# Maxima and minima taken off in PSUM by TensorE in the first K phase, with an order planned from separate pitches and latencies

## The chip, the cores and the metric

The kernel runs on one core of a Trainium2 chip. The metric is the device time of one execution in microseconds. Engines are named as the profile names them: PE (TensorE), DVE (VectorE), ACT (ScalarE), POOL (GpSimd). "The kernel before" has a median of 1112.03 us (3 runs, 1111.32 to 1113.44).

## The reference

Two layers of linear attention with a learned feature map, each followed by a gated MLP. Sequence 2048, width D = 576, 32 heads of 18 columns, MLP width 4608, bf16.

```python
def A(x, wqkv, w_phi, wo):                 # x is LayerNormed
    q, k, v = ...                          # x @ wqkv, 32 heads of 18
    pq = einsum("bhsd,hdf->bhsf", q, w_phi); pk = ...   # the same for k
    phi_q = concat([softmax(pq), softmax(-pq)])         # over the 18 columns
    phi_k = concat([softmax(pk), softmax(-pk)])
    kv = einsum("bhsf,bhsd->bhfd", phi_k, v); z = phi_k summed over s
    o  = (phi_q @ kv) / (phi_q @ z + 1e-6)
    return o @ wo
def B(x, w_gate, w_up, w_down):
    return ((x @ w_gate) * (x @ w_up)) @ w_down
x = x + A(ln(x)); x = x + B(ln(x)); x = x + A(ln(x)); x = x + B(ln(x))
```

softmax(-pk) needs the minimum where softmax(pk) needs the maximum. So each tile of 128 rows needs, for each of 32 heads, a maximum, a minimum, two exponentials, two sums, and two products with the reciprocals.

## The kernel before

The kernel folds w_phi into the K and Q weights. It then works on tiles of 128 rows: LayerNorm, transpose, projections of K, V and Q, softmax of K, and products with V that add up in three PSUM banks. After the last K tile, DVE copies that sum through a mask into SBUF (the "masked copy" of the K/V state), and only then can Q tiles be finished. The MLP of layer 1 starts when the first two Q tiles (Q0 and Q1) have gone through the whole attention. Q projections of later tiles can be done early, as filler in idle PE time, or later inside the MLP.

The softmax front of one tile:

```python
def softmax_front(self, st_, pz, Wm, km, crit, ...):
    ...                                       # two PSUM banks, projection on PE
    for h in range(2):                        # ACT copies the tile to SBUF
        ... e.copy(psb[:, pz, 288*h:288*h+288], s.ps[:, bank, 0:288])
    ops = [Op(665, ... tensor_reduce(mxmn[:, pz, 0, :], p3, AX.X, ALU.max))]   # DVE, from SBUF
    for h in range(2):
        ops.append(Op(370, ... tensor_reduce(mxmn[...], pv, AX.X, ALU.min)))   # DVE, from PSUM
    yield ("ops", "dve", ops)
    yield ("alt", [(eng, [Op(dur, ... tensor_tensor(d1, p3, mxb, ALU.subtract))])
                   for eng, dur in (("pool", 1150), ("dve", 675))[:1 + (crit > 1)]])
    ...                                       # two subtractions of the minimum: DVE, from PSUM
    yield from s.softmax_tail(sm, crit, pz)   # 2 exps (ACT), sum (DVE), reciprocal, 2 products:
                                              # the same ("pool", 1150), ("dve", 675) alternatives
```

The order of instructions on each engine is not written down: a list scheduler inside the kernel's Python makes it. Each `Op` carries a price in ns; the scheduler books it on its engine when its inputs are ready by the plan. An engine then runs its instructions in that order, whatever the real durations are. An "alt" may go to the engine where the plan has it done earlier; `crit > 1` (K tiles 14 and 15) adds DVE as an alternative for products that are GpSimd's otherwise.

```python
SEM_LAT = 64.0          # one wait between any two engines
...
    f = self.fin.get(d, 0.0) + (PE_SELF if eng == "pe" and d[0] == "pe" else SEM_LAT)
...
    fin = t + o.dur     # the price, as given in the Op
```

## Time and profile before

I cut the execution into four stretches, by PE's timeline: up to the first gate/up matmul of MLP 1, MLP 1 up to the first Wq matmuls after its last down matmul, the layer boundary up to the first gate/up matmul of MLP 2, and the rest.

| stretch, kernel before | from | to | length, us |
|---|---|---|---|
| first stretch (K phase and first Q tiles) | 0 | 116.65 | 116.65 |
| MLP 1 | 116.65 | 617.40 | 500.75 |
| layer boundary | 617.40 | 650.64 | 33.24 |
| MLP 2 and end | 650.64 | 1109.5 | 458.9 |

PE is full in the MLP stretches. Work taken out of them shortens the time directly.

### The profile page before, as it was taken

The page shows a single profiled execution, that of the slowest core. Times are in us where ns is not written, and L with a number is a line of the kernel's source. Part 1 is how long each engine was busy: PE and PEld are TensorE (multiplying, and loading weights), DVE is VectorE, ACT ScalarE, POOL GpSimd, SP SyncE. Part 2 cuts the span into 40 slices and gives each one's busy share as a digit, 9 for nine tenths or more (in the row PEclk, how much of TensorE's full clock was granted, in tenths as well). Part 3 has the DMA queues.
Part 4 walks back from the last instruction along what each step waited for, and adds up shares of the span by engine and source line. Part 5 has one row for each costly group of instructions (what it writes and reads, how often), then busy time and mean ns, then how long its engine had stood idle before and what let it go on. Part 6 is the DMA issues. An engine that isn't in the chain of part 4 may idle for free.

```text
span 1109.5 us, 33782 instructions
## 1 busy us (share of the span) xinstructions
PE 1072.4 (97%) x15342; PEld 832.2 (75%) x15342; DVE 586.1 (53%) x1192; ACT 373.7 (34%) x855; POOL 311.4 (28%) x330
## 2 busy tenths in 40 slices
PE   6787999999999999999999899999999999999998
PEld 4565886868687786869687678696969696969685
DVE  8998744646375564636453675444435353524231
ACT  6776631414133242404232463131313130402120
POOL 4885512414152432413220252211212130300000
PEclk9999999999999999999999999999999999999999
DMA  7595227273552616371523313727172726262504
GB/s 169 121 279 194 38 44 195 48 205 47 149 100 78 162 29 194 48 204 27 159 69 96 98 24 47 215 36 216 36 215 35 205 47 188 63 182 48 180 26 140
DMA packets 185002, 129.07 MB, mean 116 GB/s; under 512 B 103322, under 2 KB 183706, under 8 KB 183706
## 3 DMA queue, kind: packets, MB, share of 16 engines
q1 hardware_dynamic: 184858, 126.91, 44.6%
q8 instruction: 120, 1.97, 0.7%
q14 instruction: 24, 0.20, 0.1%
HBM read 100.75 MB, written 2.36 MB: 93 GB/s over the span
## 4 chain that ended last, share of the span: by engine, by line
PE 87%; DVE 4%; DMA 1%; ACT 1%; POOL 1%; issue 0%
PE ps L1428 50%; PE ps L1501 22%; PE ps L1002 7%; PE ps L1503 3%; PE ps L990 2%; PE ps L1289 2%; PE ps L1170 1%; DVE ss L1117 1%; POOL dd L1128 1%; DVE x_sb L1364 1%; DMA oT<-dd 1%; DMA wdr<-in_B_w_down_dram 0%; DMA wdx<-in_B_w_down_dram 0%; DVE mxmn L1035 0%; DVE dd L1049 0%
## 5 line engine op out<-in xcount | busy, mean ns | idle before, releaser
L1428 PE MATMUL ps<-xT,Wu 64*128 64x256 bf16 x4608 | 581.8, 269 | 0.0
L1428 PE MATMUL ps<-xT,Wg 64*128 64x256 bf16 x4608 | 579.2, 269 | 0.8 <-ACT xT L972 0.8
L1428 PEld LDWEIGHTS ps<-xT,Wu 64*128 64x128 bf16 x4608 | 431.5, 94 | 22.0 <-DVE hT L1476 0.3
L1428 PEld LDWEIGHTS ps<-xT,Wg 64*128 64x128 bf16 x4608 | 427.4, 94 | 27.4 <-issue 3.3
L1474 ACT CAST hT<-ps 128x512 bf16<-128x512 f32 x288 | 168.4, 585 | 568.5 <-PE ps L1428 541.7
L1476 DVE TENSOR_TENSOR hT<-ps,hT 128x512 bf16<-128x512 f32 x288 | 198.3, 690 | 240.7 <-ACT hT L1474 238.9
L1501 PE MATMUL ps<-wdr,hT 128*128 128x512 bf16 x960 | 245.2, 380 | 1.0 <-DMA wdr<-in_B_w_down_dram 1.0
L1503 PE MATMUL ps<-wdr,hT 128*128 128x64 bf16 x960 | 185.0, 193 | 0.0
L1428 PE MATMUL ps<-xT,Wr 64*128 64x256 bf16 x1152 | 184.9, 269 | 0.0
L1501 PEld LDWEIGHTS ps<-wdr,hT 128*128 128x128 bf16 x960 | 93.9, 98 | 111.1 <-DMA wdr<-in_B_w_down_dram 1.8
L1128 POOL TENSOR_TENSOR dd<-dd,ss 128x576 bf16<-128x576 bf16 x119 | 137.1, 1174 | 123.0 <-ACT ss L1124 119.0
L1099 POOL TENSOR_TENSOR dd<-xT,mxq 128x576 bf16<-128x576 bf16 x56 | 63.5, 1163 | 329.4 <-DVE mxq L1095 329.4
L1544 DVE TENSOR_TENSOR x_sb<-ps,x_sb 128x64 bf16<-128x64 f32 x32 | 7.0, 220 | 228.6 <-PE ps L1503 228.6
L962 POOL TENSOR_SCALAR xln<-x_sb,nmean,rstd 128x576 bf16<-128x576 bf16 x100 | 61.1, 616 | 182.1 <-ACT rstd L951 103.7
L1503 PEld LDWEIGHTS ps<-wdr,hT 128*128 128x128 bf16 x960 | 94.1, 98 | 0.2
L1117 DVE TENSOR_REDUCE ss<-dd 128x64 f32<-128x1152 bf16 x61 | 81.9, 1344 | 15.1 <-ACT dd L1111 15.0
L1428 PEld LDWEIGHTS ps<-xT,Wr 64*128 64x128 bf16 x1152 | 78.1, 94 | 5.2
L1501 PE MATMUL ps<-wdx,hT 128*128 128x512 bf16 x192 | 54.3, 380 | 0.1
L1109 ACT ACTIVATE dd<-dd 128x576 bf16<-128x576 bf16 x61 | 41.7, 684 | 32.8 <-DVE dd L1049 22.7
L1040 POOL TENSOR_TENSOR dd<-psb,mxmn 128x576 bf16<-128x576 bf16 x26 | 30.3, 1166 | 64.8 <-DVE mxmn L1030 64.8
L934 DVE BATCH_NORM_STATS2 st<-x_sb 128x6 f32<-128x288 bf16 x120 | 45.9, 444 | 2.4 <-DMA x_sb<-in_A_x_dram 2.4
L1002 PE MATMUL ps<-Wo,oT 64*128 64x288 bf16 x504 | 44.0, 283 | 1.2 <-DMA oT<-dd 0.4
(123 smaller groups left out, 970.0 us busy)
## 6 DMA issues: line engine op xcount, KB each, us to landing
wdr<-in_B_w_down_dram SPq DMA_DIRECT2D x240, 288.0 KB, 3.7
wdx<-in_B_w_down_dram SPq DMA_DIRECT2D x48, 288.0 KB, 3.7
Wg<-in_B_w_gate_dram SPq DMA_DIRECT2D x4, 1152.0 KB, 17.0
Wu<-in_B_w_up_dram SPq DMA_DIRECT2D x4, 1152.0 KB, 19.5
x_sb<-in_A_x_dram SPq DMA_DIRECT2D x8, 288.0 KB, 3.4
out_dram<-x_sb SPq DMA_DIRECT2D x16, 144.0 KB, 2.7
Wraw<-in_A_wqkv_dram SPq DMA_DIRECT2D x8, 144.0 KB, 2.8
xT<-xln SPq DMA_TRANSPOSE x58, 2.6
```

What stands on the lines that cost most here:

```text
L934: ops.append(Op(d_dve(288), (lambda e, j=j, h=h, src=src: e.bn_stats(st[:, sl[j], 6 * h:6 * h + 6], src)), reads=rd, writes=[("st", sl[j], ...
L962: em = [(lambda e, j=j, a=a, b=b, c=c: e.tensor_scalar(xln[:, sl[j], a:b], x_sb[:, ss[j], c:c + b - a], s.nmean[:, sl[j]:sl[j] + 1], rstd[ ...
L1002: out.append(Op(61, (lambda e, h=h, k=k, st=(i == 0 and k == 0), sp=(i == 1 and k == 3): e.matmul(s.ps[:, banks[h], 0:N], L[r, k, :], Wm[r ...
L1099: yield ("ops", "pool", [Op(1150, (lambda e, d=d, mb=mb: e.tensor_tensor(d, p3, mb, ALU.subtract)), reads=[("xT", st_), ("mq", mq, br)], w ...
L1109: yield ("ops", "act", [Op(590, (lambda e: e.activation(de2, de2, ACTF.Exp, scale=-1.0)), reads=s.ddk(sm, 1), writes=s.ddk(sm, 1))])
L1117: Op(1320, (lambda e: e.tensor_reduce(ss[:, sm, :].rearrange("p (b g) -> p b g", b=2), e4, AX.X, ALU.add)), reads=s.ddk(sm, 0) + s.ddk(sm, ...
L1128: yield ("alt", [(eng, [Op(dur, (lambda e, ev=ev, rb=rb: e.tensor_tensor(ev, ev, rb, ALU.mult)), reads=s.ddk(sm, br) + [("ss", sm)], write ...
L1428: out.append(Op(54.3, (lambda e, bank=bank, cs=cs, lhsT=lhsT, rhs=rhs, st=st, sp=sp: e.matmul(ps[:, bank, cs].rearrange("p (a n) -> p a n" ...
L1474: yield ("ops", "act", [Op(540, (lambda e, gb=gb, p=p: e.copy(hT[:, p, :], ps[:, gb, :])), reads=[("gu", gb)], writes=[("hT", p)] + (s.raw ...
L1476: yield ("ops", "dve", [Op(625, (lambda e, ub=ub, p=p: e.tensor_tensor(hT[:, p, :], ps[:, ub, :], hT[:, p, :], ALU.mult)), reads=[("gu", u ...
L1501: ops = [Op(d_pe(512), (lambda e: e.matmul(s.ps[:, bank, 0:512], lhsT, s.wslot(slot)[:, fi, 0:512], start=(f == 0), stop=(f == NF - 1))), ...
L1503: Op(d_pe(64) + 3, (lambda e: e.matmul(s.ps[:, z, 64 * sl:64 * sl + 64], lhsT, s.wslot(slot)[:, fi, 512:576], start=(f == 0 and (sl == 0 o ...
```

## The change

The intent: DVE is the busiest engine of the first K phase. So for K tiles 0 to 13 the subtraction goes to PE. DVE takes maxima and minima of the K tile straight from PSUM into a 128-column tile `mx`; PE transposes it, ACT or DVE copies it back negated as `mxT`, and PE multiplies it with a constant matrix `E` of zeros and ones and adds that to the K tile in its own PSUM bank: for the first exponential K - max, and, since the second `E` holds the difference of the two patterns, K - min for the second. ACT's exponentials read PSUM. The SBUF copy, the subtractions of DVE and that of GpSimd go. The plan gets separate latencies for each engine, lower prices for ACT, and other knobs.

```diff
-SEM_LAT = 64.0
+LAT = {"pe": 200.0, "act": 145.0, "dve": 120.0, "pool": 90.0, "sp": 64.0}
...
 def d_act(n, psum=False, ptrs=0):
-    return n / 1.2 + (63.0 if psum else 92.0) + 93.0 * ptrs
+    return n / 1.2 + 50.0
...
+        self.pes = (0, 1, 2, 3, 4, 5, 6, 7, 8, 9, 10, 11, 12, 13)
-        self.wage = 0.0
-        self.lnage = 4
-        self.lnlead = 14
+        self.wage = 10
+        self.lnage = -3
+        self.lnlead = 7
-        self.pqp = (5, 5)
-        self.pqg = 12
-        self.NPQ = 2
+        self.pqp = (3, 3)
+        self.pqg = 10
+        self.NPQ = 3
...
+    def pe_front(self, st_, crit):
+        ...                                    # K projection into two PSUM banks
+            yield ("ops", "dve", [Op(370, ... tensor_reduce(s.mx[:, mx, c:c + 16], pv, AX.X, alu)) ...
+        yield ("ops", "pe", [Op(70, ... matmul(tp, s.mx[:, mx, :], s.ident[:], ...))])
+        yield ("alt", [... ("act", ... activation(s.mxT[:, mx, :], tp, ACTF.Copy, scale=-1.0)), ("dve", ...)])
+        for br in range(2):
+            for h in range(2):
+                ... matmul(s.ps[:, bank, 0:288], s.mxT[:, mx, :], s.E[:, br, ...], start=False, ...)
+            for h in range(2):
+                ... activation(s.dd[:, sm, br, ...], s.ps[:, bank, 0:288], ACTF.Exp, scale=1.0 - 2.0 * br)
+        ...                                    # banks released, then the old tail without its exps
```

## The prediction

> **What bounds the kernel now.** I read the page's busy totals first, then a table of busy time in stretches that I cut where the work changes, then the timelines of PE and DVE inside the first stretch. The total:
>
> ```profile
> PE 1072.4 (97%) x15342; PEld 832.2 (75%) x15342; DVE 586.1 (53%) x1192; ACT 373.7 (34%) x855; POOL 311.4 (28%) x330
> ```
>
> TensorE is busy for 97% of the 1109.5 us span, so the change can only win PE's idle time, or PE work. The stretches say where that idle time is. Columns: busy us of PE, PEld, DVE, ACT, POOL with instruction counts, then clock, DMA share and GB/s.
>
> ```profile
> 0.00:116.65 116.65, 89.60 (x760) 64.10 (x762) 101.95 (x221) 82.09 (x219) 75.00 (x84) 0.97 0.65 182
> 116.65:150.00 33.35, 33.19 (x584) 29.47 (x585) 22.96 (x41) 15.47 (x35) 15.46 (x14) 1.00 0.28 47
> 150.00:610.00 460.00, 459.50 (x6896) 354.96 (x6891) 242.27 (x498) 144.50 (x330) 134.12 (x144) 1.00 0.45 110
> 610.00:655.00 45.00, 39.86 (x396) 29.25 (x396) 29.41 (x62) 24.48 (x62) 11.04 (x10) 1.00 0.21 63
> 655.00:1080.00 425.00, 424.50 (x6432) 338.57 (x6430) 183.80 (x364) 104.26 (x206) 75.76 (x80) 1.00 0.45 115
> 1080.00:1109.50 29.50, 25.78 (x288) 15.83 (x284) 5.76 (x10) 2.93 (x5) 0.00 (x0) 0.99 0.43 131
> ```
>
> At 116.65 us the first gate/up matmul of the gated MLP starts (line 1428 in PE's timeline). From there PE is full except for 5.1 us at the layer boundary and 3.7 us at the end. Of 37.1 us of idle PE, 27.0 lie before 116.65. In that first stretch DVE is the busiest, 101.95 of 116.65 us, and between 18.34 us (first maximum of a K tile) and 102.13 us (the masked copy of the K/V state) its timeline has only 5.6 us of gaps. So the first K phase is DVE's. One K tile on DVE:
>
> ```profile
> 45.06 0.74 DVE L1030 TENSOR_REDUCE mxmnx<-psbx 128x32 f32<-128x576 bf16 x1
> 45.72 0.81 DVE L1035 TENSOR_REDUCE mxmnx<-ps 128x16 f32<-128x288 f32 x2
> 46.47 1.35 DVE L1117 TENSOR_REDUCE ss<-dd 128x64 f32<-128x1152 bf16 x1
> 47.74 0.81 DVE L1049 TENSOR_TENSOR dd<-ps,mxmnx 128x288 bf16<-128x288 f32 x2
> 48.47 0.74 DVE L1030 TENSOR_REDUCE mxmnx<-psbx 128x32 f32<-128x576 bf16 x1
> ```
>
> Start to start, not end to start, is what an instruction costs here: 0.66 us for the maximum, 0.73 for two minima, 1.27 for the sum, 0.73 for two subtractions, 3.4 us in all, to which LayerNorm comes. PE's pitches are read in the same way:
>
> ```profile
> 626.98 7.51 PE L990 MATMUL ps<-Wq,xT 128*128 128x288 bf16 x60
> 634.33 0.36 PE L1170 MATMUL ps<-vx,dd 128*128 128x152 bf16 x3
> ...
> 120.59 0.78 PE L1002 MATMUL ps<-Wq,xT 64*128 64x288 bf16 x10
> 121.20 0.27 PE L1428 MATMUL ps<-xT,Wg 64*128 64x256 bf16 x1
> ```
>
> 7.35 us for 60 is 0.1225 us per full-array matmul of 288 columns; 0.61 us for 10 is 0.061 per half-array one.
>
> **What the Trainium skill says.** "VectorE: DVE Perf Modes", the perf-mode tier table, lists tensor_reduce at 1x for every operand kind. The trace agrees: 576 bf16 elements from SBUF at a 0.66 us pitch are 1.15 ns per element, and 288 fp32 from PSUM at 0.365 us are 1.27, so moving the maximum from SBUF to PSUM costs little (0.73 against 0.66). "Perfetto Trace Analysis", identifying the most-contended engine, warns that matmul busy time is no measure of headroom, since matmuls overlap. The trace agrees, ten matmuls of 1.39 us busy start every 1.23 us, so I count PE work in pitches. "TensorE: Matmul & The Clock Gate", what's actually happening, says that PE's clock halves after an idle window of about 3.4 us. The trace agrees: after PE's idle 3.39 us before 32.76 us, ten Wk matmuls took 2.19 us instead of 1.39. Fewer long gaps would therefore also save a little there.
>
> **The change part by part.** It applies to tiles 0 to 13 of layer 1's K; tiles 14 and 15, all Q tiles and layer 2 keep the old front.
>
> DVE loses, per tile, the 0.66 us maximum and two subtractions (0.73), and gets two maxima from PSUM (0.73). Net 0.66 us, times 14: 9.2 us. The 0.73 us of subtraction are not won: they pay for the maxima.
>
> GpSimd loses its subtraction, 1.166 us in the row of line 1040; the built order has 20 of them against 35, so 17.5 us go, and three small set-up operations come, some 3 us while it waits anyway. ACT loses two copies (about 0.29 us pitch) and two 576-wide exponentials (0.58) per tile, and gets four 288-wide exponentials (an estimate from the copies: 0.29 to 0.33) and a 128-wide negation (about 0.2): about even. Neither is the bound at 82 and 75 us.
>
> PE gets, per tile, one 128-wide transpose by matmul (about 0.08 us from the existing transposes, 6 in 0.49) and four 288-wide matmuls: 14 x (0.08 + 4 x 0.1225) = 8.0 us.
>
> The new plan also moves work; this I take from the instruction order of the built kernels. Before the first gate/up matmul the changed kernel has 160 Wq matmuls instead of 110, and three state products of 12 matmuls instead of two. A Q tile costs 10 x 0.1225 = 1.23 us there and 18 x 0.061 = 1.10 us in the MLP, so five tiles and one product (0.62 us) take 6.7 us into the first stretch and 6.1 us out of the saturated one. The whole program has 336 Wq matmuls instead of 392, and a tile moved to the full array saves 8 of them, so seven tiles move: two more in layer 2, 2.2 us out of the saturated MLP, 2.5 us into the boundary or just before it, where 5.1 us of PE are idle; I book a net gain of 1 us.
>
> **The sum for the first stretch.** PE's pitched work from 13.1 us (first V projection) on, before: 454 matmuls of 288 x 0.1225 = 55.6; 16 K/V products x 0.61 = 9.8; state products 1.3; transposes 3.0; folding of Wq 1.6; together 71.3 of 103.55 us, 69%. After: 71.3 + 8.0 + 6.7 = 86.0.
>
> DVE between first K maximum and masked copy, before: 83.8 - 5.6 gaps = 78.2 us. After: minus 9.2, minus one sum of a Q tile that now comes later (1.3), plus one subtraction that the plan gives DVE (1.25), plus a Wq copy and two negations (0.8): 69.8. With the same gaps the masked copy comes 8.4 us earlier, at 93.7. I do not believe in the same gaps. A tile's exponentials now wait for DVE reduce, PE transpose, ACT copy, PE matmul; both PSUM banks are held through all this, and only five banks are free beside the three of the K/V state, so two tiles fill them almost. PE would have to run near 85% in that time. I add 2.5 us: masked copy at about 96.
>
> From there to the MLP, before, it took 14.5 us, with 11.5 us of PE work after the copy. The plan now puts eight Q tiles there instead of four and a third product: 4.9 + 0.6 = 5.5 us more, of which some 1 us falls into gaps of the chain. 96 + 14.5 + 4.5 = 115. So the MLP starts only 1.7 us earlier, but with 6.1 us less to do.
>
> Total: -1.7 - 6.1 - 1 = -8.8 us, from 1112.0 to 1103.
>
> **The rivals.** (a) PE becomes the bound of the first phase: with 8 us of new work in dependent pieces, in order, it stalls on ACT's exponentials. For it: the chain above and the banks. Against it: 71.3 of 103.55 us leave 32 us. If the gaps on DVE double to 11 us, the MLP starts at about 118 and the time is 1106 to 1107. (b) The plan fits so well that DVE's gaps stay at 5 us or shrink and PE is denser: MLP at 111 or 112, time 1099. For it: separate pitches and latencies describe what the timeline shows (0.81 us duration, 0.73 pitch for two), where the old plan had one wait constant for all engines. (c) The MLP's start is set by its weights, not by the K phase, so that an earlier end is worth nothing: in the DMA rows by time they flow at about 400 GB/s from some 65 to 93 us. The changed plan has the last LayerNorm at about the same share of DVE's work, some 3 to 5 us later in time, so they would land near 97, still before 115. I give it little. (d) The first stretch is faster and the saturated MLP loses it again through reordered evictions: PE is at 99.9% there with DVE 53% and ACT 31% busy, so there is slack; 1 to 3 us at most.
>
> **Range and chances.** The gain is bounded: even if all 27 us of early idle went, 5 of them are the wait for the first weights, and 8 us of new PE work eat a third of the rest. A gain over 2% needs 22 us; it would need a first phase with no gaps at all. A loss over 2% would need the MLP to start 29 us later than I expect. The range 1096 to 1109 spans rival (b) at its best and (a) at its worst.
>
> **What would show it right or wrong.** DVE busy before the first gate/up matmul should be about 97 us in spite of the extra Q work (101.95, minus 9.2, plus some 4.5 moved in: a third state product's divisions, copies and two more sums); DVE gaps from the first K maximum to the masked copy should be 6 to 11 us; that copy should be at 94 to 99, the MLP's start at 112 to 118; the two MLP stretches should be shorter by about 6 and 2 us. I am wrong if the waits of PE on ACT's exponentials or of DVE's sum on them exceed about 10 us in all, if the MLP's first matmul waits for a weight DMA, or if the MLP stretches do not shrink.

## The result, and the profile after

The changed kernel took 1109.17 us in the median (4 runs, 1107.88 to 1110.21), beside 1111.7 for the kernel before in the same rounds. The ratio is 0.9974, 95% interval 0.9956 to 0.9991. The gain is a quarter of a per cent, 2.5 us by the medians instead of 9, and the time lies 0.2 us outside the predicted range. The profiled execution spans 1108.5 us against 1109.5. It is the slowest of the four of the changed kernel, and the profiled one of the kernel before (1111.19 us) was faster than that kernel's other runs, so the stretches below show 1.0 of the 2.5 us.

The busy totals of the changed kernel:

```profile
PE 1074.4 (97%) x15294; PEld 827.0 (75%) x15356; DVE 579.8 (52%) x1180; ACT 369.4 (33%) x870; POOL 297.5 (27%) x318
```

DVE is 6.3 us less busy and GpSimd 13.9; PE is as full as it was. The table of busy time in stretches (columns as in the prediction):

```profile
0.00:119.18 119.18, 100.88 (x892) 75.20 (x893) 99.49 (x217) 83.78 (x252) 65.08 (x75) 1.00 0.64 180
...
150.00:610.00 460.00, 455.55 (x6796) 352.81 (x6822) 242.94 (x494) 141.33 (x321) 132.01 (x141) 1.00 0.46 111
610.00:655.00 45.00, 40.84 (x403) 30.33 (x403) 28.59 (x60) 25.98 (x66) 13.91 (x12) 1.00 0.19 59
```

The MLP starts 2.5 us later, not 1.7 earlier, and PE was 11.3 us busier before it. (Of PE's 4.5 us below full in the second row, a part is missing records: the group of the down matmuls has 912 of 960.) The lengths of the stretches:

| stretch | before | after | difference | predicted |
|---|---|---|---|---|
| first stretch | 116.65 | 119.18 | +2.53 | -1.7 |
| MLP 1 | 500.75 | 496.38 | -4.37 | -6.1 |
| layer boundary | 33.24 | 35.57 | +2.33 | -1 with the next row |
| MLP 2 and end | 458.9 | 457.4 | -1.5 | (in the row above) |
| span | 1109.5 | 1108.5 | -1.0 | -8.8 |

Four other runs with the same K tiles (experiments 3, 9, 10 and 13) start the K projection of tile 15 at 78.96 to 79.57 us; here it is 79.47, so this profile's K phase is no odd one.

The K tile itself became what was intended. Its new DVE work in DVE's timeline (start, duration, instruction; `x4` are two maxima and two minima):

```profile
44.50 1.34 DVE L1166 TENSOR_REDUCE ss<-dd 128x64 f32<-128x1152 bf16 x1
45.76 1.53 DVE L1086 TENSOR_REDUCE mxx<-ps 128x16 bf16<-128x288 f32 x4
47.22 0.66 DVE L956 TENSOR_SCALAR nmean<-mv 128x2 f32<-128x2 f32 x1
```

Start to start, the sum is 1.26 and the four reductions 1.46 us, 2.7 us for a tile instead of 3.4. The first reduction of K tile 14 (still on the old front) came at 76.28 us; before, at 82.94. That is 6.7 us earlier. The masked copy came at 95.99 us, where the prediction had put it (96), after 7.8 us of DVE gaps (predicted 6 to 11). So the loss lies after the K tiles. DVE's timeline there, first of the kernel before, then of the changed one:

```profile
82.94 0.74 DVE L1030 TENSOR_REDUCE mxmnx<-psbx 128x32 f32<-128x576 bf16 x1
...
93.20 1.35 DVE L1117 TENSOR_REDUCE ss<-dd 128x64 f32<-128x1152 bf16 x1
...
95.66 2.55 DVE L1117 TENSOR_REDUCE ss<-dd 128x64 f32<-128x1152 bf16 x2
98.13 1.26 DVE L1128 TENSOR_TENSOR ddx<-ddx,ssx 128x576 bf16<-128x576 bf16 x1
```

```profile
76.28 0.75 DVE L1039 TENSOR_REDUCE mxmn<-psb 128x32 f32<-128x576 bf16 x1 [1.29 <-ACT psb L1036]
...
84.79 1.71 DVE L1177 TENSOR_TENSOR ddx<-ddx,ssx 128x576 bf16<-128x576 bf16 x1
...
92.36 1.72 DVE L1177 TENSOR_TENSOR dd<-dd,ss 128x576 bf16<-128x576 bf16 x1
94.00 1.34 DVE L1166 TENSOR_REDUCE ss<-dd 128x64 f32<-128x1152 bf16 x1
...
95.99 1.95 DVE L1287 TENSOR_TENSOR BD<-ps,mask 128x456 bf16<-128x456 f32 x3
97.86 1.34 DVE L1166 TENSOR_REDUCE ss<-dd 128x64 f32<-128x1152 bf16 x1
```

The last sum in each fence is that of Q1; the sums at 93.20 and at 94.00 are those of Q0. From tile 14's first reduction to the end of Q1's sum it took 15.2 us before (82.94 to 98.13) and 22.8 us after (76.28 to 99.12), and DVE had no gap in either. The 7.6 us are work that the new plan puts in front of Q1's sum: two products at 1.64 us each from start to start (before, they came after it or on GpSimd), the three masked copies (1.87), one more K sum (1.27), one more reciprocal (0.46), one copy of folded Wq (0.49); together 7.4. The head start of 6.7 us was spent: Q0's sum ended 0.8 us later than before (95.26 instead of 94.47) and Q1's 1.0 us later.

PE's timeline from there, first before, then after:

```profile
103.55 0.98 PE L1289 MATMUL ps<-BD,eT 128*128 128x152 bf16 x12
...
106.68 0.80 PE L1289 MATMUL ps<-BD,eT 128*128 128x152 bf16 x12
...
110.64 1.39 PE L990 MATMUL ps<-Wo,oT 128*128 128x288 bf16 x10
...
116.65 0.28 PE L1428 MATMUL ps<-xT,Wg 64*128 64x256 bf16 x1
```

```profile
101.36 0.79 PE L1342 MATMUL ps<-BD,eT 128*128 128x152 bf16 x12 [0.97 <-ACT eT L1318]
...
107.51 0.78 PE L1342 MATMUL ps<-BD,eT 128*128 128x152 bf16 x12
...
112.56 1.39 PE L999 MATMUL ps<-Wo,oT 128*128 128x288 bf16 x10
...
117.23 0.79 PE L1342 MATMUL ps<-BD,eT 128*128 128x152 bf16 x12
...
119.18 0.28 PE L1481 MATMUL ps<-xT,Wg 64*128 64x256 bf16 x1
```

The first two lines of each are the products of Q0 and of Q1 with the K/V state, the third is Q1's Wo; after it, a third tile's state product stands before the MLP. Q0's product comes 2.2 us earlier than before, although PE waits 0.97 us for ACT's copy of its exponentials (`eT`). Q1's comes 0.8 us later: it starts 6.15 us behind Q0's instead of 3.13, and Q0's Wo (106.28 us in PE's timeline) now stands in front of it. Q1's Wo then falls back by 1.9 us and the MLP by 2.5. Counted from the end of Q1's sum, it took 18.5 us to the MLP before and 20.1 after; with the 1.0 us above this is the same 2.5 us.

At the boundary the changed kernel has 140 Wq matmuls on PE instead of 120. The two more tiles take 2.45 us, and the idle time there fell only from 4.3 to 4.1 us.

### The profile page after: what moved, and what is told of

It is laid out like the page before. It is cut to its first block, busy times and chain, and to the rows that moved or that the text cites. A ratio compares the mean times of both kernels' runs of the same rounds, so it can differ in the third digit from the quotient of the medians.

```text
span 1108.5 us, 33749 instructions
## 1 busy us (share of the span) xinstructions
PE 1074.4 (97%) x15294; PEld 827.0 (75%) x15356; DVE 579.8 (52%) x1180; ACT 369.4 (33%) x870; POOL 297.5 (27%) x318
## 4 chain that ended last, share of the span: by engine, by line
PE 85%; DVE 8%; DMA 2%; ACT 2%; POOL 1%; issue 1%; SPq 0%; POOLq 0%; DVEq 0%
PE ps L1481 49%; PE ps L1554 20%; PE ps L1011 6%; PE ps L1556 4%; PE ps L999 3%; PE ps L1342 2%; DVE st L943 1%; DMA wdr<-in_B_w_down_dram 1%; DVE ss L1166 1%; PE ps L1219 1%; DVE mxx L1086 1%; POOL dd L1177 1%; DVE mxmn L1044 1%; DVE hT L1529 1%; DVE mxmn L1039 1%
## 5 line engine op out<-in xcount | busy, mean ns | idle before, releaser
L1554 PE MATMUL ps<-wdr,hT 128*128 128x512 bf16 x912 | 237.0, 380 | 2.0 <-DMA wdr<-in_B_w_down_dram 2.0
L1481 PE MATMUL ps<-xT,Wr 64*128 64x256 bf16 x1152 | 174.5, 269 | 0.0
L971 POOL TENSOR_SCALAR xln<-x_sb,nmean,rstd 128x576 bf16<-128x576 bf16 (+1 forms) x99 | 60.7, 618 | 204.5 <-DVE nmean L956 107.2
L1481 PEld LDWEIGHTS ps<-xT,Wr 64*128 64x128 bf16 x1152 | 71.9, 94 | 6.6
L1554 PE MATMUL ps<-wdx,hT 128*128 128x512 bf16 x178 | 51.6, 380 | 0.9 <-DMA wdx<-in_B_w_down_dram 0.9
L1158 ACT ACTIVATE dd<-dd 128x576 bf16<-128x576 bf16 x49 | 33.5, 684 | 37.9 <-DVE dd L1058 27.5
L999 PE MATMUL ps<-Wq,xT 128*128 128x288 bf16 x300 | 40.1, 286 | 1.4 <-DVE dd L1058 1.4
L1011 PE MATMUL ps<-Wo,oT 64*128 64x288 bf16 x504 | 40.0, 283 | 0.0
## 6 DMA issues: line engine op xcount, KB each, us to landing
Wg<-in_B_w_gate_dram SPq DMA_DIRECT2D x4, 1152.0 KB, 13.1
```

The costliest lines, as they stand in the source:

```text
L971: em = [(lambda e, j=j, a=a, b=b, c=c: e.tensor_scalar(xln[:, sl[j], a:b], x_sb[:, ss[j], c:c + b - a], s.nmean[:, sl[j]:sl[j] + 1], rstd[ ...
L999: full = [Op(d_pe(N), (lambda e, k=k, h=h: e.matmul(s.ps[:, banks[h], 0:N], L[:, k, :], Wm[:, k, N * h:N * h + N], start=(k == 0 and fresh ...
L1011: out.append(Op(61, (lambda e, h=h, k=k, st=(i == 0 and k == 0), sp=(i == 1 and k == 3): e.matmul(s.ps[:, banks[h], 0:N], L[r, k, :], Wm[r ...
L1481: out.append(Op(54.3, (lambda e, bank=bank, cs=cs, lhsT=lhsT, rhs=rhs, st=st, sp=sp: e.matmul(ps[:, bank, cs].rearrange("p (a n) -> p a n" ...
L1554: ops = [Op(d_pe(512), (lambda e: e.matmul(s.ps[:, bank, 0:512], lhsT, s.wslot(slot)[:, fi, 0:512], start=(f == 0), stop=(f == NF - 1))), ...
```

## The experiments

Kernels of one call shared the runs of the kernel before (medians 1111.0 to 1111.9 us). "MLP start" is read from PE's timeline of the profiled execution. Where an edit keeps the order, the order of the changed kernel was compared and is the same on every engine. Theory names in the expectations: P and D are PE's order and DVE with the softmax chain as what holds the first stretch; the others are explained where they stand.

**1. Less PE work in the K tiles, same order.** Wrong (max and min are taken off only 64 columns; the result still passed the tolerance of the comparison).

```diff
-  s.ps[:, bank, 0:288], s.mxT[:, mx, :], s.E[:, br, 16*h:16*h+16, :]...
+  s.ps[:, bank, 0:64],  s.mxT[:, mx, :], s.E[:, br, 16*h:16*h+16, :]...[:, 0:64]
```

> The changed kernel with the same instruction order, but each of its 56 matmuls with E writes 64 of 288 columns (results wrong on purpose). At 2.4 columns per ns (0.1225 us per 288) that takes about 56 x 0.093 = 5.2 us from PE and nothing from DVE or ACT. Theory P (PE, in order and some 88% dense from 22 to 82 us, sets when the first K phase ends): the MLP starts 3 to 5 us earlier than 119.2, time 1104 to 1106. Theory D (DVE and the softmax chain of the last K and first Q tiles set it): MLP start and time move by less than 1.5 us.

1109.5 us, ratio 0.9974 (0.9954 to 0.9993). MLP start 118.10, 1.1 us earlier, for some 5.3 us of PE work less (224 of 288 columns of each of the 56 matmuls, at 0.1225 us per 288). PE's new work is not what holds the first stretch, so theory P falls.

**2. Less DVE work in the K tiles, same order.** Wrong (minima over 2 of 18 elements).

```diff
-  e.tensor_reduce(s.mx[:, mx, c:c + 16], pv, AX.X, alu)
+  e.tensor_reduce(s.mx[:, mx, c:c + 16], pv[:, :, 0:18 if c < H else 2], AX.X, alu)
```

> The changed kernel with the same instruction order, but the 28 minima of tiles 0 to 13 read 2 of each 18 elements (results wrong on purpose), about 28 x 0.26 = 7 us less DVE before 76 us, PE work unchanged. Theory P: MLP start and time gain less than 2 us. Theory D: they gain 4 to 7 us, time 1102 to 1105.

1109.21 us, 0.9971 (0.995 to 0.9992). MLP start 117.58, 1.6 us earlier; the DVE gaps before the masked copy rose from 7.8 to 11.8 us, so most of what was saved became waiting. Theory D had 4 to 7 us, so it falls too.

**3. Five Q projections put off until the MLP.** Tiles 11 to 15 wait for a signal that the MLP's start gives.

```diff
+            if st_ >= 11:
+                yield ("wait", "mlp")
```

> The changed kernel, but the Q projections of tiles 11 to 15 of layer 1 are held back until the MLP has started, so they run there as half-array matmuls as in the kernel before (5 x 1.10 us in, 5 x 1.23 us out of the first phase). Theory P (PE has no room before the MLP, moved work costs what it weighs): MLP starts 4 to 6 us earlier, at 113 to 115, the first MLP stretch is 5 to 6 us longer, time within 1.5 us of the changed kernel. Theory D (they filled idle PE): MLP start earlier by under 2 us, time 3.5 to 5.5 us longer, about 1113.

1115.3 us, 1.0025 (1.0003 to 1.0047). MLP start 118.30: 6.1 us of PE work less, 0.9 us won, as theory D had it; the time is some 2 us over its 1113. PE's timeline of this run before the MLP:

```profile
112.46 1.40 PE L999 MATMUL ps<-Wo,oT 128*128 128x288 bf16 x10
...
116.91 0.57 PE L979 MATMUL ps<-ident,xln 128*128 128x128 bf16 x6 [3.06 <-DVE xln L971]
...
118.30 0.39 PE L1483 MATMUL ps<-xT,Wg 64*128 64x256 bf16 x1
```

Where the moved tiles had been, PE now stands idle 3.06 us for LayerNorm: the end of the first stretch is a chain across engines, and the moved tiles had filled its holes. Q1's Wo (112.46 us) did not come earlier than in the changed kernel (112.56), though two of the five tiles had stood before it. MLP 1 became 501.24 instead of 496.38 us, so a moved tile is worth 4.86 / 5 = 0.97 us there.

**4. The old front under the new plan.** All tiles on the old front, everything else as changed (and the second lent SBUF slot that the old front uses).

```diff
-        self.pes = (0, 1, 2, ..., 13)
+        self.pes = ()
```

> The changed kernel's planner constants and settings, but no tile takes the PE front (all 16 K tiles as before, one spare psb slot more). Separates front from planning. If the front does the work: MLP start 3 to 8 us later than 119, time 1112 to 1117. If the planning alone gave the gain: time 1107 to 1110.

1123.46 us, 1.0106 (1.0082 to 1.0129), MLP start 126.82; the time is above all that was expected. The new plan without the new front loses 11.6 us; the front is worth 14 us inside this plan.

**5. Both light edits at once, same order** (wrong). Theory B: each engine covered for the other. Theory T: the order of the tail and the Q chain hold the end.

> Both light edits at once in the changed kernel's order: the 56 PE matmuls that take max and min off stream 64 of 288 columns, and the 28 minima read 2 of 18 elements. Wrong on purpose. Theory B (balanced: each engine covers for the other, so only lightening both shows): the MLP starts at 115.0 us or earlier (119.18 in the changed kernel, 118.10 and 117.58 with one edit alone), time 1105 to 1106. Theory T (the tail's order and the old-front Q chain set it; work taken off the K tiles is lost there): at most the sum of the two single gains, MLP at 116.5 to 118, time 1107 to 1109.

1107.23 us, 0.9965 (0.9951 to 0.9979), MLP start 117.71: not earlier than with the DVE edit alone. Part of that is the run: its first K projection started at 17.41 us, in the others at 16.8. Counted from there the two edits won 2.0 us, beside 1.1 and 1.6 alone, but B needs 4.2. B falls. In the changed kernel and in all three light ones, the time from the last K projection's start to the MLP is 39.7 us (79.47 to 119.18, 78.40 to 118.10, 77.87 to 117.58, 78.00 to 117.71): the tail is rigid, and K tiles made 5 us cheaper on PE or 6 us on DVE end only 1 to 1.6 us earlier. What holds the K tiles instead was not found.

**6. Q0 and Q1 ahead of the last K tiles.**

```diff
-        self.prio0 = (6, 7)
+        self.prio0 = (10, 7)
```

> One constant: the start age of the first two Q tiles of layer 1 is 10 instead of 6, so their projections, maxima and exponentials stand ahead of the last K tiles' sums on DVE. Theory T (the order of the tail gave the gain back): the MLP starts 2 to 4 us earlier than in the changed kernel, at 115 to 117; as fewer Q tiles are planned before it, the time moves less, 1106 to 1109. Theory R (the re-planning as a whole costs, not this piece of it): MLP start within 1 us of 119.2, time 1109 to 1112.

1111.27 us, 0.9995 (0.9977 to 1.0012). MLP start 115.07, 4.1 us earlier, as theory T had it. But the plan then did five Q tiles and one state product fewer before it; experiment 3 puts the five tiles at 0.9 us, which leaves some 3 us for the order and that product (0.6 us). The masked copy came 3.2 us later (99.21 us) and the MLP earlier all the same, so in the changed kernel it is not this copy that holds the end. MLP 1 took 501.5 us, and the time was worse than expected. An early start with fewer tiles done is no gain by itself.

**7. The new front under the old plan** (prices, waits and knobs of the kernel before).

> Only the new front of the K tiles; all planned durations, the one wait constant of 64 ns and all the planner's knobs are those of the kernel before. The old front under the new plan took 1123.5 us, 11.6 over the kernel before, and the new front under the new plan 14 less than that. Theory R (the re-planning costs what the front wins, the two are independent): 1112 minus 14, 1098 us, masked copy of the state at about 90, MLP start at about 110. Theory J (front and plan only work together; old waits of 64 ns let the planner put the new chain's pieces too close on PE): 1108 to 1114 us, MLP start 117 to 121.

1112.87 us, 1.0018 (1.0006 to 1.003); last K projection 88.42 (81.10 before the change), MLP start 119.00. Theory J: front and plan only work together. Neither half of the change wins anything alone.

**8. Corrected prices and all K tiles on the new front.** DVE's alternative costs 1400 ns in the plan, early PE work twice its price, the folding of Wq starts one tile later.

```diff
-  (("pool", 1150), ("dve", 675))          +  (("pool", 1150), ("dve", 1400))
-  fin = t + o.dur                         +  fin = t + o.dur * (2.0 if eng == "pe" and t < 20000.0 else 1.0)
-  self.fq = 3                             +  self.fq = 4        # and pes = (0, ..., 15)
```

> Attempt at a better version: all 16 K tiles use the new front, the DVE form of the normalising products is priced 1400 ns in the plan instead of 675 (the trace has 1.71 us), PE work before 20 us is planned at half speed, and one knob of the Q tiles goes from 3 to 4. Theory T (order of the tail, mis-priced products): no 1.7 us product on DVE between the last K sums, MLP start 115 to 117, time 1104 to 1107. If the mis-pricing has no part in it: MLP start 119 or later, time 1109 or more.

1107.7 us, 0.9969 (0.9955 to 0.9982); MLP start 115.55. The start is as expected. The time is 0.7 us above its range, and its interval overlaps that of the changed kernel, so a gain over that kernel is not shown.

**9. The two DVE products of the tail on 72 of 576 columns, same order** (the result is wrong). One execution.

```diff
-  lambda e, ev=ev, rb=rb: e.tensor_tensor(ev, ev, rb, ALU.mult)
+  lambda e, ev=ev[:, 0:4 if eng == "dve" else H, :], rb=...: e.tensor_tensor(ev, ev, rb, ALU.mult)
```

> The changed kernel in its own order; only the normalising products that the plan put on DVE (two in layer 1's tail, 1.71 and 1.72 us each, booked at 0.675) work on 72 of 576 columns. Wrong on purpose. Theory T1 (these two products on the chain of the tail carry the loss): about 1.4 us less each, the first Q tile's sum 2 to 2.9 us earlier, the MLP starts at 116.3 to 117.2 instead of 119.18. Theory T2 (the tail is held by PE's order of Q0's and Q1's pieces and by what follows them, not by DVE): MLP at 118.5 or later. The time follows the MLP's start: 1106 to 1107, or 1109.

MLP start 118.11, 1.07 us earlier: between the two theories. The reason is in its DVE timeline:

```profile
84.77 1.19 DVE L1177 TENSOR_TENSOR ddx<-ddx,ssx 128x72 bf16<-128x72 bf16 x1
```

With an eighth of the columns it still took 1.19 us. The two products became 0.52 us shorter each, and 1.04 us arrived at the MLP in full. So these products count one to one, but most of a product's 1.71 us is not its own work.

**10. Also the sums of K tiles 14 and 15 over 2 of 18 elements, same order** (the result is wrong). One execution.

> As the run before, and the sums of K tiles 14 and 15 also read only 2 of 18 elements (1.27 us each booked, about 0.15 left). Wrong on purpose. Theory T1 (DVE's work in the tail is the chain): another 1 to 2.2 us, MLP at 114.5 to 116. Theory T2: no further gain, within 0.5 us of the run before.

MLP start 116.43. The two sums lost 1.06 us each (1.34 to 0.28), and the MLP came 1.7 us earlier than in experiment 9, less than theory T1 had. Of this, 0.5 us was there before the first changed instruction (tile 14's first reduction came at 75.77 us instead of 76.25), so 1.2 of the 2.1 us arrived; DVE lost the rest to a wait of 0.42 us for ACT and to a subtraction that took 1.11 us instead of 0.69. DVE in the tail is on the chain. All later DVE work moves together in these two runs, so they do not tell which piece of it holds the end. Both runs stand beside experiments 1, 2 and 5, where work taken from the K tiles did not arrive.

**11. Corrected prices alone.** The first two lines of experiment 8, nothing else.

> The changed kernel planned with honest prices only: 1400 ns instead of 675 for the DVE form of the products and subtractions, PE work before 20 us at twice its time; no knob changed. Theory H (wrong prices in the plan are the cause): no 1.7 us product on DVE in the tail, MLP at 115 to 117, time 1105 to 1107. Theory K (honest prices alone move the work elsewhere, and it takes the right order too): MLP at 119 to 121, time 1108 to 1111.

1111.93 us, 1.0005 (0.9988 to 1.0021); MLP start 119.65. Theory K: honest prices do not help by themselves. No product is left on DVE in this tail, but the plan put other work there: the sum of the second of the two Q tiles stands at 100.27 us, behind the masked copy (94.11).

**12. Corrected prices and the later folding of Wq** (experiment 8 without the new front for tiles 14 and 15).

> Honest prices and one knob: the folding of Wq begins after K tile 4 instead of 3; tiles 14 and 15 keep the old front. Against the run with all 16 tiles on the new front (1107.7 us, MLP at 115.55) it tells what that part was worth. If the order (knob) does it: MLP at 115 to 117, time 1106 to 1109. If the new front for tiles 14 and 15 does it: MLP at 118 to 120, 1109 to 1111.

1108.37 us, 0.9967 (0.9949 to 0.9985); MLP start 117.83, between the two expectations. Of experiment 8's 3.6 us of earlier start, 1.3 came with the order and 2.3 with the two tiles, if single profiled starts are read so closely (the last section says why they should not be).

**13. GpSimd's products for K tiles 14 and 15 on 72 columns, same order** (the result is wrong). One execution.

> The changed kernel in its own order; the two products that GpSimd does for K tiles 14 and 15 at the same time as DVE's work on 72 of 576 columns instead; DVE's own are whole. Wrong on purpose. Theory W (DVE's product waits for GpSimd's to end): the first DVE product takes 0.75 to 0.9 us instead of 1.71; the second, beside which GpSimd also runs a whole subtraction, falls less or not at all; MLP at 117.5 to 118.5. Theory S (the two share bandwidth or the product is slow by itself): both stay at 1.4 us or more, MLP at 119.

In the changed kernel GpSimd worked beside DVE's two products like this:

```profile
84.34 1.55 POOL L1177 TENSOR_TENSOR ddx<-ddx,ssx 128x576 bf16<-128x576 bf16 x1 [0.22 <-DVE ssx L1170]
...
92.30 1.16 POOL L1049 TENSOR_TENSOR dd<-psb,mxmn 128x576 bf16<-128x576 bf16 x1
```

GpSimd's ends are 84.34 + 1.55 = 85.89 and 93.46; DVE's products end 0.6 us later each, at 86.50 and 94.08. In the run with the short GpSimd product:

```profile
84.44 0.69 POOL L1177 TENSOR_TENSOR ddx<-ddx,ssx 128x72 bf16<-128x72 bf16 x1 [0.22 <-DVE ssx L1170]
84.89 0.85 DVE L1177 TENSOR_TENSOR ddx<-ddx,ssx 128x576 bf16<-128x576 bf16 x1
```

The same DVE product took 0.85 instead of 1.71 us. The second took 1.22, ending 0.61 us after GpSimd's subtraction there. MLP start 117.91; from tile 15's K projection to the MLP it took 1.37 us less, and the two DVE products 1.36. Theory W: DVE's product waits for GpSimd's to end. In experiment 8 DVE came first, and GpSimd waited:

```profile
84.01 0.76 DVE L1177 TENSOR_TENSOR ddx<-ddx,ssx 128x576 bf16<-128x576 bf16 x1
84.05 1.73 POOL L1177 TENSOR_TENSOR ddx<-ddx,ssx 128x576 bf16<-128x576 bf16 x1 [1.87 <-DVE ssx L1170]
```

The Trainium skill states this in "SBUF — State Buffer", section "Who interferes with whom": a DVE instruction with two inputs in SBUF contends with a GpSimd instruction that reads SBUF, and the lock on the shared ports is exclusive. The traces agree with both sentences: 0.76 us alone, 1.71 behind GpSimd, 1.19 even for an eighth of the columns.

**14. A better version with many Q tiles.** The plan was searched again, off the chip, for knobs under corrected prices (DVE's alternative at 1700 ns).

```diff
+  prices as in experiment 8, with ("dve", 1700)
-  pes = (0, ..., 13)                      +  pes = (0, ..., 12, 14, 15)
-  pqp = (3, 3), NPQ = 3, qlead = 8        +  pqp = (4, 4), NPQ = 4, qlead = 12
+  two of the four Q slots are held back in layer 2
```

> Attempt at a better version: DVE's product priced 1700 ns in the plan, early PE work at twice its time, K tile 13 instead of 14 and 15 on the old front, four slots for early Q projections in layer 1 and two in layer 2 (as before the change), two other planner knobs. If honest prices let the plan keep the K phase's gain: MLP at 114 to 116 with as many Q tiles before it as in the changed kernel, the boundary 1 to 2 us shorter than its 35.6, time 1103 to 1106. If the gain is lost whatever the order: MLP at 118 or more, 1108 or more.

1104.22 us (5 runs, 1101.1 to 1105.39), ratio 0.9931 (0.9918 to 0.9944). MLP start 116.80 (0.8 us above the expected range), MLP 1 494.9, boundary 34.02, then 457.9 us. It has no product on DVE in the tail.

**15. A better version with few Q tiles.**

```diff
+  prices as in experiment 14
-  pes = (0, ..., 13)                      +  pes = (0, ..., 12)
-  pqp = (3, 3), NPQ = 3                   +  pqp = (5, 5), NPQ = 2
-  qcrit = False, sub2pool = False         +  qcrit = True, sub2pool = True
```

> The same prices, with few Q tiles before the MLP: K tiles 13 to 15 on the old front, two slots for Q projections, the first Q tiles given the extra DVE alternative. If the K phase's gain can be kept: MLP at 110 to 112.5, its first stretch about 501 us long as in the kernel before, time 1105 to 1108. If not: MLP at 115 or more, time 1110.

1105.07 us, 0.9937 (0.9922 to 0.9952). MLP start 112.58, as expected slightly above; MLP 1 501.1, boundary 34.01. It does as many Wq matmuls before the MLP as the kernel before, so I read its 4.1 us of earlier start as the K phase's gain, kept. The end of its first stretch on PE:

```profile
111.19 0.57 PE L979 MATMUL ps<-ident,xln 128*128 128x128 bf16 x6 [0.68 <-DVE xln L971]
112.58 0.28 PE L1481 MATMUL ps<-xT,Wg 64*128 64x256 bf16 x1 [0.81 <-ACT xT L981]
```

Here PE waits for the chain, and no state product of another tile stands before the MLP.

**16. The same knobs with the old prices.**

> The changed kernel with the four knobs of the version that reached 1105.1 us (K tiles 13 to 15 on the old front, two slots for early Q projections and their old priority, the extra DVE alternative for the first Q tiles), but with the prices of the changed kernel (675 ns, early PE work at full speed). If the corrected prices are needed: the order differs, the MLP starts at 117 or later and the time is 1109 or more. If the knobs alone do it: MLP at 112 to 114, 1104 to 1106.

1113.01 us, 1.0017 (1.0002 to 1.0032), MLP start 120.54. With wrong prices the same knobs give a kernel 8 us slower. So the corrected prices are necessary with these knobs, and by experiment 11 not sufficient. The two corrections, of DVE's alternative and of early PE work, were not tried apart.

**17. Experiment 14 without holding Q slots back in layer 2.**

> The version that reached 1104.2 us without its limit of two Q slots in layer 2, so four. If slots set the boundary: it takes 36.5 to 38 us instead of 34.0, with 160 Wq matmuls or so in it, and the second MLP stretch is 1 to 2 us shorter; time 1105 to 1107. If not: boundary at 34 to 35, time 1104.

1108.76 us (expected 1105 to 1107), 0.9979 (0.9962 to 0.9997). The boundary took 36.88 us instead of 34.02, as the theory of slots said, and PE was idle in it for 5.5 us instead of 2.9. It has the same 140 Wq matmuls there, not 160; only their places differ. MLP 2 did not become shorter for it (459.3 us against 457.9), which was expected and did not happen; why is open.

## Why the prediction was right or wrong

**Right: what DVE, PE and GpSimd lose and get in a K tile.** 2.7 us of DVE a tile instead of 3.4, PE pairs of the new matmuls at a 0.245 us pitch, the masked copy at 95.99 us for a predicted 96, the DVE gaps of 7.8 us inside 6 to 11. DVE's busy time before the MLP was 99.5 us for a predicted 97. That the copy is met to 0.01 us is luck: the 1.25 us booked for one more subtraction on DVE measured 0.02 (0.66 and 0.61 for two, 1.25 for one before), and the two products, which the prediction did not count, take 1.3 us more than before.

**Wrong: the step "From there to the MLP, before, it took 14.5 us ... 96 + 14.5 + 4.5 = 115".** It took 23.2 us. The step measured the tail from the masked copy, as if that copy held it. Before, that fitted: Q0's sum had ended 7.7 us before the copy, and Q0's state product started 1.4 us after the copy's start (102.13 to 103.55). In the changed order Q0's sum ended 0.7 us before the copy, and what PE waited for was the rest of Q0's chain (GpSimd's products, transposes, ACT's copy `eT`): the state product started 5.4 us after the copy's start (95.99 to 101.36). Q1's sum, which had ended 4.0 us before the copy, now ended 3.1 us after it; the prediction had noted that ("one sum of a Q tile that now comes later") and had left the tail as it was. So the 14.5 became 18.5 us, 3.95 of the 4.2 us by which the MLP's start was missed. The 4.5 us for more PE work behind it measured 4.7 (13.1 us from Q0's state product to the MLP before, 17.8 after). Its size was right and its reason only in part: experiment 3 took 6.1 us of that PE work out and won 0.9.

Q0 and Q1, which stay on the old front, so set the end, and the new order puts 7.4 us of other DVE work ahead of Q1's sum, which used up the 6.7 us of head start. Experiments 9, 10 and 13 show that DVE work there counts (the products one to one, the sums for 1.2 of 2.1 us), experiments 1, 2 and 5 that work in the K tiles mostly does not, and experiment 6 that with Q0 and Q1 in front the copy holds the end again, 1.4 us before Q0's state product, and the MLP comes 4.1 us earlier. Part of it is a price: the plan books 675 ns for a product that takes 1.64 us from start to start behind GpSimd (experiment 13), and it put two such products on DVE's chain. The rest is what the plan chose to put first: without any product there (experiment 11) the start was no earlier.

**Mis-sized: "five tiles and one product ... 6.1 us out of the saturated one".** MLP 1 became 4.4 us shorter. Five tiles alone are worth 4.86 us by experiment 3 (0.97 us each, where the step had 1.10). Beside this, the two groups of 512-column down matmuls in the page have 2.9 us of idle time in front of them instead of 1.1, nearly all put down to weight DMAs. That this comes from the change was not tested.

**Wrong in sign: "I book a net gain of 1 us" for two more tiles in layer 2.** Boundary and MLP 2 together became 0.8 us longer. The tiles did not fall into the idle time, which is at the LayerNorm of the second half. In PE's timeline before, then after, between these transposes:

```profile
646.80 2.62 PE L990 MATMUL ps<-Wq,xT 128*128 128x288 bf16 x20
649.26 0.56 PE L970 MATMUL ps<-ident,xln 128*128 128x128 bf16 x6
```

```profile
647.40 1.40 PE L999 MATMUL ps<-Wq,xT 128*128 128x288 bf16 x10
649.74 0.57 PE L979 MATMUL ps<-ident,xln 128*128 128x128 bf16 x6 [0.94 <-DVE xln L971]
```

Before, 20 Wq matmuls filled that wait; after, only 10 were left for it, and PE idled 0.94 us. The number of matmuls is not what counts: in experiment 15, with two slots, the same 140 took 34.01 us with 2.9 us of idle. Experiment 17, again with 140, shows that the number of slots moves the boundary's length through their places.

**The rivals.** Rival (a), PE as the new bound with the MLP at about 118, named nearly the right start for the wrong reason: experiments 1 and 3 took 5.3 and 6.1 us from PE and won about 1. Rival (b), a plan that fits so well that PE is denser, was half true of the K phase (PE was denser, but DVE's gaps grew from 5.6 to 7.8 us) and false of the tail. Rival (c) did not happen: the first gate/up matmul waits for no weights. Rival (d) has the size, 1.7 us less out of MLP 1 than planned; its mechanism, reordered evictions, was not tested.

**The sum.** Predicted -1.7 - 6.1 - 1 = -8.8; measured in the profiled runs +2.5 - 4.4 + 0.8 = -1.0 (rounded lengths). That most of the predicted gain was there to be had is shown by experiments 14 and 15: with the same front on 15 and on 13 tiles and a better order the kernel takes 1104.2 and 1105.1 us.

## What to carry to other kernels

Follow a gain to the end of the stretch: measure the tail from the instruction that will end last in the new order, and count what the new order puts in front of it, engine by engine. Where a planner decides the order, compare its prices with the trace for the case in which two engines contend, because one wrong price can put an instruction on the chain where it costs most. Moving filler work earlier pays only while it fills holes; beyond them it is paid in full, so count both ends of the move.

## What the Trainium skill lacked or had wrong

- "SBUF — State Buffer", section "Who interferes with whom", had it right that the lock is exclusive, and I did not look there before I predicted. It lacks a number: here a DVE product of 576 bf16 columns takes 0.76 us alone and ended 0.61 us after GpSimd's instruction in 21 of the 22 cases, in the first stretches of all runs, where that had started first, up to 1.73 us long (in the other, at 85.63 us in experiment 16, it followed straight on another DVE instruction with two inputs in SBUF, took 0.73 us, and GpSimd's took 2.22); 72 columns still took 1.19.
- "TensorE: Matmul & The Clock Gate", section "What's actually happening", gives about 3.4 us of idle as the window for the clock to halve, and says that the window runs freely, so that runs differ. The traces agree that they differ. Two executions with the same order up to there had 2.87 and 2.78 us of idle before the same ten matmuls; after the shorter idle they took 1.32 us instead of 0.77, and the start of the following work fell back by 1.6 us more:

```profile
31.39 0.77 PE L1219 MATMUL ps<-vx,dd 128*128 128x152 bf16 x10 [2.87 <-POOL dd L1177]
```

```profile
31.87 1.32 PE L1219 MATMUL ps<-vx,dd 128*128 128x152 bf16 x10 [2.78 <-POOL dd L1177]
```

  So slow matmuls appeared after less idle than the window, and the length of this gap alone did not decide it. The page warns against fitting a count of slow matmuls; what it lacks is the consequence for reading a profile: these are experiments 17 and 14, whose order is the same up to the MLP, and their MLP starts differ by 1.8 us (115.04 and 116.80). One or two us between two profiled MLP starts are therefore not to be read as a cause, with the same order or another. The readings of experiments 3, 9, 10 and 13 rest on differences that also show line by line in the tail; the 1.1 and 1.6 us of experiments 1 and 2 are within this spread, which does not change what they are used for, that 5 to 6 us did not arrive.
